# Twelve attention pairs computed in the form of the later ones, with a new order of the matmul blocks around them

## The chip, the cores and the metric

One core of one Trainium2 chip runs the whole program. The metric is device time in microseconds (us) of one execution. TensorE (PE) does the matmuls, VectorE (DVE) and ScalarE (ACT) work on what it leaves in PSUM, GpSimd (POOL) prepares sums of weights, and SyncE (SP) issues nearly all transfers.

## The reference

A windowed attention over 8 batches and 8 heads, then a feed-forward layer with a parametric ReLU on its output. Heads 0 to 3 see the last 32 tokens, heads 4 to 7 every fourth of the last 128.

```python
scores = scale * np.matmul(q, k.transpose(0, 1, 3, 2))      # q, k, v: 8, 8, 576, 64
scores = np.where(masks[None], scores, -1e9)                # plain heads, dilated heads
attn = np.exp(scores - scores.max(-1, keepdims=True))
attn = attn / (attn.sum(-1, keepdims=True) + 1e-9)
x = np.matmul(attn, v)                                      # to 4608 tokens x 512
h = x @ w_in                                                # 512 x 2048
g = np.maximum(h, 0) + alpha * np.minimum(h, 0)
out = g @ w_out                                             # 2048 x 512
```

## The kernel before

**Feed-forward.** Tokens come in nine tiles of 512. Each float32 factor is held as a high and a low part, and a product takes three passes (high by high, high by low, low by high). Tiles 0, 1 and 2 are done in 48 slices (t, f) of one tile by 128 columns of `w_in`; slice n = 0 to 47 is the loop variable of the file's last loops. A slice has two blocks on TensorE, each 12 matmuls of 512 columns: h(n) (`ffn_h`, line 467) and, later, y(n) (`ffn_y`, line 515). Between them stand `ffn_parts` (two DVE instructions that read h from PSUM, lines 487 and 488; for n up to 20 `ffn_sum`, line 480, in their place), `ffn_high` (one ACT cast, line 493) and `ffn_low` (one DVE subtraction, line 498). y(n) reads the high part in its first matmul and the low part from its second on. Slices 6 to 21 are tile 1, 22 to 31 tile 0, 32 to 47 tile 2. Tiles 3 to 8 are done afterwards, two tiles at a time, by `paired_stage`.

**Attention.** A pair is two heads of one batch; pair p = 0 to 31. `scores` puts the products of a pair into two PSUM banks (line 229, or line 253 in the later form), `maxima` masks them and takes row maxima (DVE, lines 288 and 291), `exponentials` is nine ACT instructions (line 301), `divisions` and `turns` normalize and transpose (DVE, lines 308 to 316), `values` multiplies by v (line 333, later form line 278), and `highs` and `lows` copy the result out of PSUM into the token tiles (ACT line 387; DVE lines 392 and 394).

**Two forms.** In the earlier form each quarter of the partitions belongs to one head and one half of the sequence, and the values go to two banks. In the later form (`mixed`, pairs 20 to 31) each quarter takes a run of one head and then a run of the other (`chain`), the values go to four banks, one for each of four runs (`CHAINS`), and the copies out of PSUM are cut by run. Three late pairs (`NARROW`) keep one head on each quarter in that form. The later form has its own masks and its own layout of v.

**Order.** Every engine works through its instructions in the order in which the program issues them. PSUM has eight banks: four "a" banks, handed out in turn by `bank("a", ...)` to h, scores and values, and four "y" banks that collect y for a whole tile. A bank is handed on when its last reader is done. Up to n = 18 DVE and ACT also convert the weights (lines 429 to 448). In the loop of line 1505 pair p = 8 to 19 has its scores at n = 20 + 2(p - 8), its divisions at the next slice and its values at the slice after that (pair 8 one later), so that from n = 24 to 42 the order on TensorE is: h, y, scores, values, h, y. Every second odd slice also splits a sum of weights (`combined_high`, `combined_low`, line 578). From n = 39 on the operands of `paired_stage` are prepared from token tiles 3 and 4 (`token_parts`, lines 659 to 674, put into `late_ops` at 39, 43, 45, 46 and 47). After the loop come y(47), the four copies of tile 2's result (`end`, lines 525 and 527), and `paired_stage`, whose first six matmuls are followed by the scores of pair 20, into two of the y banks just emptied.

Of the kernel before, what the change touches and what calls it, by code (L numbers as in the profile page):

```python
# [18 lines left out]
B, H, S, D = 8, 8, 576, 64  # L19
# [14 lines left out]
NSTD = 3  # L34
NFP = NF // 2
AHEAD = 20
EARLY = 20
NARROW = (27, 28, 31)
GP = 4
# [28 lines left out]
def tile_window_attention_prelu_ffn(  # L68
# [110 lines left out]
    class Pair:  # L179
        def __init__(self, b, c):  # L180
            self.b, self.c = b, c
            p = b * NC + c
            self.onto = p <= NC + 2
            self.small = nc.gpsimd if p <= NC else nc.vector
            self.banks = "y" if self.onto else "a"
            self.late = p == 0
            self.plain = 2 * c < HP
            self.mask = PLAIN if self.plain else DILATED
            self.id = f"{b}_{c}"
            self.pr = spare_pr[p % 2] if b < 2 else pr0  # L190
            self.room = rooms[c] if b < 2 else None
            self.sm = sums[p % 2]
            self.mixed = p >= AHEAD
            self.narrow, self.tags, self.spots = p in NARROW, None, None

        def load_qk(self):
# [9 lines left out]
        def load_v(self):  # L206
            if self.room is None:
                self.v = att.tile([P, HB + 1 + self.mixed, D], F32, tag="v", name=f"v_{self.id}")
            else:
                self.v = self.room[:, 2 * S:taken].rearrange("p (j d) -> p j d", d=D)  # L210
            nc.sync.dma_start(out=self.v, in_=vX[self.b - AHEAD // NC, self.c] if self.mixed else vW[self.b, self.c])

        def scores(self):

# [123 lines left out]
        def places(self):  # L338

            base = self.b * S  # L340
            if self.mixed:
                for n, (first, length) in enumerate(CHAINS):
                    a, last = first * BQ, (first + length) * BQ
                    flat = self.po[n].rearrange("d i q -> d (i q)")
                    while a < last:
                        if self.plain:
                            t = (base + a) // TT
                            z = min(last, (t + 1) * TT - base)
                            to = half(t, self.c)[:, base + a - t * TT:base + z - t * TT]
                        else:  # L350
                            r, i = divmod(a, SEG)
                            t = (base + i * DILATION) // TT
                            z = min(last, r * SEG + min(SEG, ((t + 1) * TT - base) // DILATION))
                            i -= (t * TT - base) // DILATION
                            to = half(t, self.c).rearrange("d (i r) -> d r i", r=DILATION)[:, r, i:i + z - a]
                        yield n % 2, flat[:, a - first * BQ:z - first * BQ], [to]
                        a = z
                return
            for u in range(2):
                flat = self.po[u].rearrange("d i q -> d (i q)")  # L360
                if self.plain:
                    a, end = base + u * HQ, base + (u + 1) * HQ
                    while a < end:
                        t = a // TT
                        z = min(end, (t + 1) * TT)
                        s0 = a - base - u * HQ
                        x, cut = half(t, self.c), slice(a - t * TT, z - t * TT)
                        yield u, flat[:, s0:s0 + z - a], [x[:, e, cut] for e in range(2)] if t < NSTD else [x[:, cut]]
                        a = z
                else:  # L370
                    src = flat.rearrange("d (r i) -> d i r", r=2)
                    a, end = base, base + S
                    while a < end:
                        t = a // TT
                        z = min(end, (t + 1) * TT)
                        i0, i1 = (a - base) // DILATION, (z - base) // DILATION
                        x, cut = half(t, self.c), slice(a - t * TT, z - t * TT)
                        yield u, src[:, i0:i1], [
                            p.rearrange("d (i r) -> d i r", r=DILATION)[:, :, 2 * u:2 * u + 2]
                            for p in ([x[:, e, cut] for e in range(2)] if t < NSTD else [x[:, cut]])]  # L380
                        a = z
# [933 lines left out]
        w.magnitude()  # L1315
        return w

    def masks_of(kind):
        nc.sync.dma_start(out=mask_sb[:, kind:kind + HB], in_=masks[:, kind:kind + HB])

    def behind(t, *lots):

# [97 lines left out]
            load()  # L1420

    sums_early = {}
    loads_early = {CUT - 2: [lambda: masks_of(PLAIN)]}
    for k in range(GP):
        first, last = early_sum(k)
        loads_early[CUT + 4 * k - 3 if k else NC - 1] = [first]
# [66 lines left out]
    for p in range(2 * NC, AHEAD):  # L1493
        n = EARLY + 2 * (p - 2 * NC)
        score_at[n] = pairs[p]
        value_at[n + 3 if p == 2 * NC else n + 2] = pairs[p]
    divide_at = {n + 1: u for n, u in score_at.items()}

    split_at, combine_at = {}, {}
    for k in range(NFP):  # L1500
# [3 lines left out]

    for n in range(CUT, NS):
        scored, valued, divided = (at.get(n) for at in (score_at, value_at, divide_at))
        whole = n + 1 == 2 * NF
        if n + 1 < NS and not whole:
            ffn_h(*slices[n + 1])
        if n <= SECOND - 2:  # L1510

# [5 lines left out]
            for op in words[:1]:  # L1517
                op()
            ffn_low(*slices[n])
            if divided and n < SECOND - 2:  # L1520
                divided.divisions()
                divided.turns()
            for op in words[1:]:
                op()
            if n + 1 <= SECOND - 2:
# [6 lines left out]
                w.high()  # L1532
        elif late:
            late.pop().low()
        if whole:
            ffn_y(*slices[n - 1])
            ffn_h(*slices[n + 1])
        if SECOND - 2 <= n < NS - 1:
            ffn_parts(*slices[n + 1])
            ffn_high(*slices[n + 1])  # L1540
            if divided:
                divided.divisions()
                divided.turns()
            ffn_low(*slices[n + 1])
        if valued is pairs[2 * NC]:
            valued.values()
            valued.highs()
            valued.lows()
        if not whole:
            ffn_y(*slices[n - 1])  # L1550
        if n in split_at:
            combined_high(split_at[n])
        if scored:
            scored.scores()
        if valued and valued is not pairs[2 * NC]:
            valued.values()
        if n in split_at:
            combined_low(split_at[n])
        if scored:
            scored.maxima()  # L1560
            scored.exponentials(0, 5)
        while ended:
            ended.pop()()
        if valued and valued is not pairs[2 * NC]:
            valued.highs()
            valued.lows()
        if scored:
            scored.exponentials(5)
        for u in pairs[2 * NC:AHEAD + 1]:
            if u is pairs[2 * NC]:  # L1570
                due = 2 * (n == SECOND - 4,)
# [11 lines left out]
            combine(combine_at[n], "xB1" if n < SCRATCH + 5 else "xA1")  # L1583
        if n == NS - 9:
            plan_parts()
        if n == NS - 2:
            nc.sync.dma_start(out=mask_sb, in_=masks[:, NMASK:2 * NMASK])
        for op in late_ops.pop(n, ()):
            op()
        if n >= NS - NRING + 2:  # L1590
# [81 lines left out]
```

## Time and profile before

| | |
|---|---|
| median of 3 runs | 846.46 us (846.22 to 846.62) |
| the profiled execution | 846.51 us |
| its span, first to last instruction | 844.3 us |
| PE busy | 828.9 us (98%) |
| DVE busy | 629.7 us (75%) |
| ACT busy | 446.6 us (53%) |

Times in the rows below are counted from the start of that span. A timeline row gives start, duration, engine, line, operation, output <- input, and how many like instructions were merged into it; in square brackets stands idle time ahead of it and who ended it. The duration of a merged row holds the tail of its last matmul, so the pace of TensorE is read from one row's start to the next one's.

### The profile page before, as it was taken

Reading aid. Unit: us, or ns where it says so; the run is one execution under the profiler, and the core shown is the slowest. Engines: PE = TensorE matmul, PEld = TensorE weight load, DVE = VectorE, ACT = ScalarE, POOL = GpSimd, SP = SyncE. Lnnn points to the kernel's source line nnn. Section 1 sums busy time; section 2 is a strip of 40 time slices with the busy share of each in tenths; the row PEclk is TensorE's granted clock in tenths of the full one; section 3 lists DMA queues with packets and bytes.
Section 4 is the critical chain, followed back from the end, with each engine's and each line's share of the span. In section 5 each row is a group of like instructions: output and inputs, shape, how many; then the busy total and the mean of one; then the engine's idle time right before and its main releaser. Section 6 shows DMA issues by size and latency. Waiting matters only on the chain.

```text
span 844.3 us, 20355 instructions
## 1 busy us (share of the span) xinstructions
PE 828.9 (98%) x8071; PEld 675.2 (80%) x8071; DVE 629.7 (75%) x1043; ACT 446.6 (53%) x1234; POOL 126.6 (15%) x146
## 2 busy tenths in 40 slices
PE   8899999999999999999999999999999999999998
PEld 5577888888888888878778888788888888888886
DVE  4988788986767677697645987888379978843983
ACT  6886676444333444566436652666266446634650
POOL 0205154700314350040630000000000000000000
PEclk9999999999999999999999999999999999999999
DMA  7766567635989976577887678767766786667673
GB/s 250 255 200 190 200 224 229 196 103 176 293 268 313 307 229 213 194 218 242 269 306 211 196 215 284 221 194 212 222 168 191 219 265 196 190 197 192 193 216 136
DMA packets 123966, 185.59 MB, mean 220 GB/s; under 512 B 10464, under 2 KB 64352, under 8 KB 123872
## 3 DMA queue, kind: packets, MB, share of 16 engines
q1 hardware_dynamic: 123584, 184.03, 70.8%
q8 instruction: 64, 1.05, 0.5%
q10 hardware_dynamic: 288, 0.26, 0.1%
q14 instruction: 30, 0.25, 0.1%
HBM read 138.12 MB, written 46.14 MB: 218 GB/s over the span
## 4 chain that ended last, share of the span: by engine, by line
PE 90%; DVE 4%; ACT 3%; DMA 2%; issue 1%; SPq 0%; ACTq 0%; DVEq 0%
PE h L467 15%; PE y L515 15%; PE pA L681 14%; PE qA L1118 12%; PE pC L681 7%; PE qC L1118 6%; PE y L964 6%; PE qB L1118 3%; PE pB L681 3%; PE o L333 2%; PE s L229 2%; PE s L253 1%; PE o L278 1%; ACT w_dt.float L301 1%; DMA w_dt.float<-qT 1%
## 5 line engine op out<-in xcount | busy, mean ns | idle before, releaser
L467 PE MATMUL h<-x,w_dt.float32r 128*128 128x512 f32 x576 | 143.0, 397 | 2.1 <-DVE w_dt.float32r L448 1.1
L515 PE MATMUL y<-g,w_dt.float32r 128*128 128x512 f32 x576 | 138.8, 390 | 0.6 <-ACT w_dt.float L301 0.6
L467 PEld LDWEIGHTS h<-x,w_dt.float32r 128*128 128x128 f32 x576 | 107.8, 190 | 26.2 <-DVE w_dt.float32r L448 2.0
L515 PEld LDWEIGHTS y<-g,w_dt.float32r 128*128 128x128 f32 x576 | 107.7, 188 | 23.4 <-ACT w_dt.float L301 1.1
L301 ACT ACTIVATE pr<-pr,nm 128x64 f32<-128x64 f32 x216 | 72.3, 338 | 47.8 <-DVE nm L291 47.8
L493 ACT CAST g<-m 128x512 fp32r<-128x512 f32 x48 | 29.7, 619 | 72.2 <-DVE m L488 68.3
L681 PE MATMUL pA<-parts_w,ring_w 128*128 128x512 f32 x234 | 58.4, 391 | 0.0
L681 PE MATMUL pA<-parts_w,ring_xA 128*128 128x512 f32 x228 | 56.4, 390 | 0.0
L834 DVE TENSOR_TENSOR gp<-stage,gp 128x512 fp32r<-128x512 f32 x80 | 53.5, 683 | 3.4 <-ACT gp L830 3.4
L830 ACT CAST gp<-stage 128x512 fp32r<-128x512 f32 x80 | 46.9, 618 | 9.3 <-DVE stage L827 8.1
L681 PEld LDWEIGHTS pA<-parts_w,ring_w 128*128 128x128 f32 x234 | 43.7, 188 | 9.6 <-ACT stage L723 0.5
L681 PEld LDWEIGHTS pA<-parts_w,ring_xA 128*128 128x128 f32 x228 | 42.6, 188 | 9.0 <-ACT stage L944 0.2
L498 DVE TENSOR_TENSOR g<-m,g 128x512 fp32r<-128x512 f32 x48 | 38.2, 795 | 15.6 <-ACT g L493 15.6
L1118 PE MATMUL qA<-gp,ring_xA 128*128 128x512 f32 x192 | 46.4, 390 | 0.0
L1118 PEld LDWEIGHTS qA<-gp,ring_xA 128*128 128x128 f32 x192 | 35.9, 188 | 7.5
L301 ACT ACTIVATION_READ_ACCUMULATOR pr<-pr,nm 128x1 f32 x216 | 40.9, 189 | 0.0
L1118 PE MATMUL qA<-gp,ring_w 128*128 128x512 f32 x168 | 40.5, 389 | 0.0
L487 DVE TENSOR_SCALAR m<-h,al 128x512 f32<-128x512 f32 x27 | 20.2, 748 | 22.8 <-PE h L467 22.8
L1118 PEld LDWEIGHTS qA<-gp,ring_w 128*128 128x128 f32 x168 | 31.5, 188 | 6.5
L288 DVE SCALAR_TENSOR_TENSOR pr<-s,mask_sb 128x320 f32<-128x320 f32 (+1 forms) x48 | 21.7, 452 | 16.8 <-PE s L253 13.5
L808 DVE TENSOR_TENSOR stage<-pC,stage 128x512 f32<-128x512 f32 x25 | 17.2, 688 | 21.7 <-ACT stage L944 21.7
L1019 DVE TENSOR_TENSOR py<-qA,py 128x512 f32<-128x512 f32 x20 | 13.7, 692 | 20.7 <-PE qA L1118 20.7
(214 smaller groups left out, 1681.6 us busy)
## 6 DMA issues: line engine op xcount, KB each, us to landing
ring_w<-wS SPq DMA_DIRECT2D x68, 256.0 KB, 3.3
ring_xA<-wS SPq DMA_DIRECT2D x67, 256.0 KB, 3.7
ring_g<-wS SPq DMA_DIRECT2D x33, 256.0 KB, 2.8
wO<-w_dt.float32r SPq DMA_DIRECT2D x32, 256.0 KB, 4.7
wS<-wc SPq DMA_DIRECT2D x16, 512.0 KB, 3.6
ring_w<-wO SPq DMA_DIRECT2D x32, 256.0 KB, 3.2
ring_xA<-wY SPq DMA_DIRECT2D x32, 256.0 KB, 3.3
ring_w<-wY SPq DMA_DIRECT2D x32, 256.0 KB, 3.0
```

Of the source, the lines that this page charges most:

```text
L288: nc.vector.scalar_tensor_tensor(out=self.pr[:, a:z], in0=self.ps[i], scalar=SCALE, in1=mask_sb[:, self.mask + a:self.mask + z], op0=ALU.m ...
L301: nc.scalar.activation(out=self.pr[:, r, :], in_=self.ps[r // CUT0][:, r % CUT0, :] if self.onto else self.pr[:, r, :], func=AF.Exp, bias= ...
L467: nc.tensor.matmul(ms[t, f], lhsT=weight(0, a, f)[:, c * P:(c + 1) * P], rhs=half(t, c)[:, e, :], start=(c == 0 and n == 0), stop=(c == NC ...
L487: nc.vector.tensor_scalar(out=m, in0=ps, scalar1=0.0, scalar2=al[:, f:f + 1], op0=ALU.min, op1=ALU.mult)
L493: nc.scalar.copy(out=g[:, 0, :], in_=ms[t, f])
L498: nc.vector.tensor_tensor(out=g[:, 1, :], in0=ms.pop((t, f)), in1=g[:, 0, :].bitcast(F32), op=ALU.subtract)
L515: nc.tensor.matmul(ys[t][c], lhsT=weight(1, a, f)[:, c * P:(c + 1) * P], rhs=g[:, e, :], start=(first and n == 0), stop=(last and n == 2),)
L681: nc.tensor.matmul(to, lhsT=w[:, (2 * a + c) * P:(2 * a + c + 1) * P], rhs=part_of(name, e)[:, c * TT:(c + 1) * TT], start=start and c == ...
L830: nc.scalar.copy(out=self.pair(n)[:, 0], in_=self.whole(n))
L834: nc.vector.tensor_tensor(out=p[:, 1], in0=self.whole(n), in1=p[:, 0].bitcast(F32), op=ALU.subtract)
L964: nc.tensor.matmul(ys2[tt], lhsT=w[:, k * P:(k + 1) * P], rhs=g[:, e], start=j == 0 and n == 0, stop=j == GF - 1 and n == 2)
L1118: nc.tensor.matmul(named(to)[c], lhsT=w[:, b * P:(b + 1) * P], rhs=rhs[:, e], start=begins and k == 0, stop=i == GP - 1 and k == 2, skip_g ...
```

## The change

Pairs 8 to 19 take the later form: `MIXED = 8` takes the place of `AHEAD` where the form is chosen, and `places` writes a high and a low part where the token tile is one of the first three. The masks of that form are loaded at n = 16 and 17; the loads at n = 4 and 46 go. Divisions move to two slices after the scores, values to three after. From n = 20 on an even slice issues y(n-1) ahead of h(n+1) and then the scores; an odd slice issues h(n+1), y(n-1) and then the values.

```diff
+MIXED = 8
-            self.mixed = p >= AHEAD
+            self.mixed = p >= MIXED
...
-            nc.sync.dma_start(out=self.v, in_=vX[self.b - AHEAD // NC, self.c] if self.mixed else vW[self.b, self.c])
+            nc.sync.dma_start(out=self.v, in_=vX[self.b - MIXED // NC, self.c] if self.mixed else vW[self.b, self.c])
...
-                            to = half(t, self.c)[:, base + a - t * TT:base + z - t * TT]
+                            cut = slice(base + a - t * TT, base + z - t * TT)
...
-                            to = half(t, self.c).rearrange("d (i r) -> d r i", r=DILATION)[:, r, i:i + z - a]
-                        yield n % 2, flat[:, a - first * BQ:z - first * BQ], [to]
+                            cut = slice(r + i * DILATION, r + (i + z - a - 1) * DILATION + 1, DILATION)
+                        x = half(t, self.c)
+                        yield n % 2, flat[:, a - first * BQ:z - first * BQ], (
+                            [x[:, e, cut] for e in range(2)] if t < NSTD else [x[:, cut]])
...
-    loads_early = {CUT - 2: [lambda: masks_of(PLAIN)]}
+    loads_early = {EARLY - 4: [lambda: masks_of(PLAIN, NMASK)], EARLY - 3: [lambda: masks_of(DILATED, NMASK)]}
...
-        value_at[n + 3 if p == 2 * NC else n + 2] = pairs[p]
-    divide_at = {n + 1: u for n, u in score_at.items()}
+        value_at[n + 3] = pairs[p]
+    divide_at = {n + 2: u for n, u in score_at.items()}
...
-        whole = n + 1 == 2 * NF
-        if n + 1 < NS and not whole:
+        turned = n >= EARLY and n % 2 == 0
+        if turned:
+            ffn_y(*slices[n - 1])
+        if n + 1 < NS:
             ffn_h(*slices[n + 1])
...
-            if divided and n < SECOND - 2:
-                divided.divisions()
-                divided.turns()
...
-        if whole:
-            ffn_y(*slices[n - 1])
-            ffn_h(*slices[n + 1])
+        while turned and ended:
+            ended.pop()()
+        if divided:
+            divided.divisions()
+            divided.turns()
+        if scored:
+            scored.scores()
         if SECOND - 2 <= n < NS - 1:
             ffn_parts(*slices[n + 1])
             ffn_high(*slices[n + 1])
-            if divided:
-                divided.divisions()
-                divided.turns()
-            ffn_low(*slices[n + 1])
-        if valued is pairs[2 * NC]:
-            valued.values()
-            valued.highs()
-            valued.lows()
-        if not whole:
+            if not scored:
+                ffn_low(*slices[n + 1])
+        if not turned:
             ffn_y(*slices[n - 1])
         if n in split_at:
             combined_high(split_at[n])
+        if valued:
+            valued.values()
         if scored:
-            scored.scores()
-        if valued and valued is not pairs[2 * NC]:
-            valued.values()
+            scored.maxima()
+            ffn_low(*slices[n + 1])
+            scored.exponentials()
+        if valued:
+            valued.highs()
+            valued.lows()
+        while ended:
+            ended.pop()()
         if n in split_at:
             combined_low(split_at[n])
-        if scored:
-            scored.maxima()
-            scored.exponentials(0, 5)
-        while ended:
-            ended.pop()()
-        if valued and valued is not pairs[2 * NC]:
-            valued.highs()
-            valued.lows()
-        if scored:
-            scored.exponentials(5)
...
-        if n == NS - 2:
-            nc.sync.dma_start(out=mask_sb, in_=masks[:, NMASK:2 * NMASK])
```

The rest of the diff is the argument of `masks_of` and the layout of v on the host.

## Rows read from the trace of the kernel before

**Rows 1.** Busy time by stretch: engines, granted clock, share of DMA engines, GB/s

```profile
168.00:322.00 154.00, 154.00 (x2179) 127.42 (x2178) 109.91 (x204) 65.35 (x273) 42.49 (x45) 1.00 0.76 240
322.00:345.00 23.00, 23.00 (x173) 18.95 (x172) 19.59 (x24) 10.38 (x14) 0.00 (x0) 1.00 0.47 149
```

**Rows 2.** Timeline of TensorE, two scores that follow each other, earlier form

```profile
205.37 1.21 PE L229 MATMUL s<-k,q 64*32 64x64 f32 x72
...
218.90 1.21 PE L229 MATMUL s<-k,q 64*32 64x64 f32 x72
```

**Rows 3.** Timeline of TensorE at n = 20 and 21: h(21), y(19), scores, h(22)

```profile
159.89 3.26 PE L467 MATMUL h<-x,w_dt.float32r 128*128 128x512 f32 x12
162.99 2.89 PE L515 MATMUL y<-g,w_dt.float32r 128*128 128x512 f32 x12
165.81 1.21 PE L229 MATMUL s<-k,q 64*32 64x64 f32 x72
166.94 3.03 PE L467 MATMUL h<-x,w_dt.float32r 128*128 128x512 f32 x12
```

**Rows 4.** Timeline of TensorE in `paired_stage`, later form, scores and values apart

```profile
403.85 0.97 PE L253 MATMUL s<-k,q 64*32 64x64 f32 x72
404.75 3.06 PE L964 MATMUL y<-gp,ring_w 128*128 128x512 f32 x12
407.74 1.13 PE L278 MATMUL o<-pt,v 32*64 32x32 f32 x84
408.80 4.37 PE L964 MATMUL y<-gp,ring_xA 128*128 128x512 f32 x18
413.10 0.97 PE L253 MATMUL s<-k,q 64*32 64x64 f32 x72
```

**Rows 5.** The same timeline, the scores of a pair of `NARROW`

```profile
446.20 1.21 PE L253 MATMUL s<-k,q 64*32 64x64 f32 x72
```

**Rows 6.** Timeline of TensorE, values alone at n = 44, and the loop's end

```profile
327.17 1.35 PE L333 MATMUL o<-pt,v 32*64 32x32 f32 x76
328.45 3.01 PE L467 MATMUL h<-x,w_dt.float32r 128*128 128x512 f32 x12
...
336.74 8.32 PE L515 MATMUL y<-g,w_dt.float32r 128*128 128x512 f32 x36
...
346.35 0.97 PE L253 MATMUL s<-k,q 64*32 64x64 f32 x72
```

**Rows 7.** Timeline of DVE: the low part of slice 19

```profile
161.66 0.67 DVE L498 TENSOR_TENSOR g<-m,g 128x512 fp32r<-128x512 f32 x1
```

**Rows 8.** Timeline of TensorE: an h block that stopped after its second matmul

```profile
71.42 0.61 PE L467 MATMUL h<-x,w_dt.float32r 128*128 128x512 f32 x2
73.17 2.56 PE L467 MATMUL h<-x,w_dt.float32r 128*128 128x512 f32 x10 [1.15 <-DVE w_dt.float32r L448]
```

**Rows 9.** Timeline of DVE, n = 43 to the loop's end

```profile
320.51 0.16 DVE L308 TENSOR_TENSOR rs<-sums,tiny 128x9 f32<-128x9 f32 x1
...
322.45 0.65 DVE L498 TENSOR_TENSOR g<-m,g 128x512 fp32r<-128x512 f32 x1
...
324.15 1.22 DVE L666 TENSOR_TENSOR parts_w<-raw_xB,parts_w 128x1024 fp32r<-128x1024 f32 x1
...
328.76 0.75 DVE L487 TENSOR_SCALAR m<-h,al 128x512 f32<-128x512 f32 x1
...
331.53 0.28 DVE L394 COPY raw_xB<-o 128x128 f32<-128x128 f32 x1
...
340.50 0.69 DVE L498 TENSOR_TENSOR g<-m,g 128x512 fp32r<-128x512 f32 x1 [0.76 <-ACT g L493]
...
345.65 1.28 DVE L525 COPY ob<-y 128x512 f32<-128x512 f32 x2
```

**Rows 10.** Timeline of DVE: the five copies of a late dilated pair

```profile
443.36 0.80 DVE L394 COPY raw_xB<-o 128x16 f32<-128x16 f32 x5 [3.81 <-PE o L278]
```

**Rows 11.** The page's costliest groups: masks of a pair, two such instructions each

```profile
L288 DVE SCALAR_TENSOR_TENSOR pr<-s,mask_sb 128x320 f32<-128x320 f32 (+1 forms) x48 | 21.7, 452 | 16.8 <-PE s L253 13.5
```

More of the change, by code (lines that the diff above doesn't have):

```diff
@@ L1316, in conversion, with masks_of @@
         return w
-    def masks_of(kind):
-        nc.sync.dma_start(out=mask_sb[:, kind:kind + HB], in_=masks[:, kind:kind + HB])
+    def masks_of(kind, mixed=0):
+        nc.sync.dma_start(out=mask_sb[:, kind:kind + HB], in_=masks[:, mixed + kind:mixed + kind + HB])
     def behind(t, *lots):
@@ L1643 @@
     vw = v.reshape(B, NC, 2, 2 * HB, BQ, D)[:, :, :, blocks].transpose(0, 1, 2, 3, 5, 4, 6).reshape(B, NC, P, HB + 1, D)
-    blocked = v.reshape(B, NC, 2, 2 * HB, BQ, D)[AHEAD // NC:]
+    blocked = v.reshape(B, NC, 2, 2 * HB, BQ, D)[MIXED // NC:]
     vx, vn = (
@@ L1651 @@
     for p in NARROW:
-        at = p // NC - AHEAD // NC, p % NC
+        at = p // NC - MIXED // NC, p % NC
         vx[at] = vn[at]
```

## The prediction, made before the change was run

> **What bounds the kernel now.** I read the busy times by stretch first. From 168 to 345 us, the stretch in which pairs 8 to 19 run, TensorE is busy all the time, 154.00 of 154.00 us and then 23.00 of 23.00, at full granted clock [rows 1]. So time is won here only by making TensorE's own work shorter, and any new wait of TensorE is lost in full. The second thing to see in the same view is that DVE has 44 us to spare in the first stretch but almost none in the last 23 us of the loop, where it is busy 19.59 us [rows 1]. Then I read TensorE's timeline for the pace and the price of a pair, and DVE's timeline wherever a block is moved nearer to the work that feeds it.
>
> The pace: 36 matmuls from 336.74 to the next row, which by the same timeline starts 1.45 us before 346.35, take 8.16 us, or 0.227 us each [rows 6]. A block of 12 takes 2.72 us.
>
> **A pair on TensorE.** In the earlier form two back-to-back pairs start 13.53 us apart with four blocks (10.88 us) between [rows 2], so scores and values together cost 2.65 us; ten pairs of scores with values stand like that. Scores alone cost 1.13 us [rows 3], values alone 1.28 us [rows 6]. In the later form scores take 0.90, values 1.06 us, and a whole round with 30 matmuls (6.80 us) takes 9.25 us, so a pair costs 2.45 us although its scores and values stand apart [rows 4]. The 12 matmuls between them take 2.99 instead of 2.72 us: 0.27 us to leave small matmuls and come back, a little less around the values. That the gain comes from alternating heads, and not from the call, is seen in a pair that keeps one head on a quarter: its scores last 1.21 us, as in the earlier form, against 0.97 [rows 2, 4, 5].
>
> Now the sum. Before: ten at 2.65 = 26.5; two scores alone at 1.13 + 0.25 and two values alone at 1.28 + 0.25 add 5.8; together 32.3. After: twelve at 2.45 = 29.4. That is **2.9 us saved** (2.8 to 3.0). Four more value matmuls a pair (84 records for 76) are inside the 1.06 us [rows 4, 6].
>
> The split has a price of its own: an extra change between large and small matmuls costs some 0.25 us a pair, 1.13 + 1.28 = 2.41 us alone, 2.65 with one pair of changes, 2.9 with two [rows 2, 3, 6]. The Trainium skill, "TensorEngine Tiling (Array Packing)", section Key Properties, says that a change of tiling mode drains the engine. This trace agrees, and the twelve extra pairs of changes are already in the 2.45; without them the saving would be some 5 us.
>
> **The first turned slice, n = 20.** The old order was y(18), h(21), y(19). The new one puts y(19) straight behind y(18), at 159.89 us, where h(21) stood [rows 3]. But the low part of slice 19 is still queued on DVE behind weight conversions that the change doesn't touch: it starts at 161.66 and ends at 162.33 [rows 7]. y(19) may issue its first matmul and must then wait. A block that stops after some matmuls is seen elsewhere: two issued, then 1.15 us idle until a DVE result came [rows 8]. The second matmul was due at 159.89 + 0.23 = 160.12, so TensorE **loses 2.2 us**. Bounds: 1.8 if DVE runs a little ahead, 2.6 with the handover. What h(21) loses today at the same place, 3.10 us instead of 2.72 [rows 3], goes, since its weights are then long converted: **0.4 us back**.
>
> **The end of the loop.** Here DVE is the engine to follow [rows 1]. Today the low part of slice 47 starts at 340.50, and after it four operand instructions and the copies of y(47) follow; the first copy of the last row, half of 1.28 us, ends at 345.65 + 0.64 = 346.29, and the scores of pair 20, which need that bank, start at 346.35 [rows 6, 9]. There is no slack: what DVE is late there, TensorE waits. The change puts into this queue pair 19's divisions and transposition, which used to be done one slice earlier ahead of the operand work (322.45 - 320.51 = 1.94 us [rows 9]), and moves pair 19's values two blocks later, just ahead of y(45).
>
> I count from the end of pair 18's values. DVE: five copies, 0.15 + 0.80 [rows 10], 0.95; the low part of the weight sum, about 1.13 (of the 1.70 from 322.45 to 324.15), 2.1; the three operand instructions with a cast between, 328.76 - 324.15 = 4.61, 6.7; divisions and transposition, 1.94, 8.6; slice 45's parts, cast and low part, 331.53 - 328.76 = 2.77, 11.4; the two parts instructions of slice 46, about twice 0.75, 12.9 [rows 9]. TensorE by then has done y(43), h(45), h(46) and y(44), 4 x 2.72 + 0.23 = 11.1 us, and wants to start pair 19's values. Their four banks are, in turn, two free ones and those of h(45) and h(46). The last is free only at 12.9. **So TensorE waits 1.8 us** for a bank that the two-bank form didn't need. Values end at 13.9; y(45) and h(47) end at 19.5; DVE, which has meanwhile done three more operand instructions, takes up slice 47 at 19.7, and its low part starts 2.77 - 0.61 = 2.16 later, at 21.9. From there the old distance holds, 346.29 - 340.50 = 5.79: pair 20's scores start at 27.7. Without waits TensorE would be there after eight blocks, six matmuls, the values and four changes: 21.76 + 1.36 + 1.06 + 0.5 = 24.7. **Loss: 3.0 us.** Bounds: 1.3 if the bank is free in time and only DVE's longer queue counts; 3.7 if that queue is later by half a microsecond more.
>
> **The rest.** The masks are now two loads of 295 KB ahead of pair 8's keys and values on SP, instead of one early and a whole one at n = 46. They come behind the last weight loads in the queue, and pair 8's mask is first read some 20 us later; without that cover each would cost its 1.2 us at 240 GB/s [rows 1]. Divisions move to where DVE waits for h anyway, for all pairs but the last. Copies out of PSUM grow from 2 to 3 a side to as many as 9 for pairs 10 and 11 and 5 or 6 for the other dilated pairs; at 0.16 us each [rows 10] they cost DVE under 1.5 us of the 13 us of a round, beside y and h blocks. Both go in at nothing; the price without the cover is the third rival.
>
> **Sum.** 846.51 (the profiled execution; span 844.3 and 2.2 around it; the median is 846.46) - 2.9 - 0.4 + 2.2 + 3.0 = **848.4 us**.
>
> **Rivals.**
>
> *No new wait.* y(19)'s data or the last banks come in time after all, because DVE, with h(21) later and GpSimd's sums behind it, works faster than its rows of today. Then only the saving stands: 846.5 - 3.3 = **843.2**. It decides from the point at which DVE's low part of slice 19 ends before 160.1. Against it: that instruction is queued behind work that is issued in the same order in both kernels. Chance 0.08.
>
> *Only one of the two waits.* With the wait at n = 20 alone, 845.4; with the end of the loop alone, 846.2. For it: my count of the end runs over a dozen queued steps, and half a microsecond of slack in h(46)'s bank would shorten it by about that. Chance 0.22.
>
> *The four banks catch every round.* In a steady round, counted from the end of values, y(n-1) and h(n+1) take 2 x 2.72 and two changes, so slice n+1's parts can start at 5.8 us, the four mask and maximum instructions take some 1.8 [rows 11], the low part 0.6, and slice n+2's parts end at about 11.1; the next values, after scores and two more blocks, start at 12.2. That is a margin of 1.1 us. If DVE is late by more, as it is when GpSimd slows it, each of eleven rounds pays the excess: 0.3 us each gives 848.4 + 3.3 = **851.7**. The Trainium skill, "TensorEngine Tiling (Array Packing)", section PSUM Bottleneck, names this outcome: tiling speeds up TensorE and not the evacuation of PSUM. No row shows it in the loop so far. Chance 0.13.
>
> **How the numbers follow.** Forecast 0.53, rivals 0.08, 0.22 and 0.13, and 0.04 for what I don't see. The forecast's own range, from its bounds, is 846.3 to 849.6. The range of 8 in 10 takes in the second rival below and the light cases of the third above: **845.4 to 850.0**. A measurement of this kernel tells about 0.2% from no change, 1.7 us, so faster is under 844.8 and slower over 848.2. The forecast lies just over that line: three fifths of it, the third rival and half of the unseen are slower, 0.45; the rest of the forecast and the second rival are within, 0.43; the first rival and a remainder are faster, 0.12.
>
> **What would show it.** In the changed kernel's timeline of TensorE: scores of 0.97 and values of 1.13 us for all of pairs 8 to 19; y(19) split after its first matmul with some 2 us idle, released by DVE's low part; a wait in pair 19's values released by the parts of slice 46; a wait before or in pair 20's scores released by a copy of y(47). If TensorE is busy without gaps from 168 to 345 us, the first rival is right; if values wait in many rounds, the third. I am wrong altogether if values in four banks take longer here than in the later stage.

## The result, and the profile after

| | before | after |
|---|---|---|
| median of 4 runs | 846.34 us (845.71 to 846.62) | 856.82 us (856.17 to 858.36) |
| profiled execution | 846.51 us, span 844.3 | 856.63 us, span 854.8 |
| forecast | | 848.4 us (845.4 to 850.0) |

The ratio is **1.0127** (95%: 1.0110 to 1.0145). The kernel became slower, as forecast, but by 10.5 us and not by 2: the time lies outside the range.

The lines that answer to [rows 1], busy time by stretch (PE, PEld, DVE, ACT, POOL, then granted clock, share of the DMA engines, GB/s), in the kernel after:

```profile
168.00:322.00 154.00, 149.00 (x2173) 119.61 (x2168) 112.89 (x218) 62.69 (x277) 47.07 (x48) 0.98 0.76 235
322.00:345.00 23.00, 21.73 (x253) 17.68 (x252) 18.53 (x34) 11.02 (x38) 0.00 (x0) 1.00 0.48 153
```

TensorE, which had no gap in either stretch, now has five microseconds in the first and 1.3 in the second. Where they lie is read from its timeline. First a quiet round, which answers to [rows 2] (scores, then values, then the next scores):

```profile
192.42 0.97 PE L254 MATMUL s<-k,q 64*32 64x64 f32 x72
...
198.99 1.13 PE L279 MATMUL o<-pt,v 32*64 32x32 f32 x84
...
205.71 0.97 PE L254 MATMUL s<-k,q 64*32 64x64 f32 x72
```

A round lasts 13.29 us, against 13.53 in [rows 2]. The new form works, with scores and values as long as in [rows 4].

The two places that the prediction named. At n = 20, which answers to [rows 3, 7] (TensorE, then DVE's low part of slice 19):

```profile
157.06 3.49 PE L518 MATMUL y<-g,w_dt.float32r 128*128 128x512 f32 x13
161.69 2.79 PE L518 MATMUL y<-g,w_dt.float32r 128*128 128x512 f32 x11 [1.14 <-DVE g L501]
```
```profile
160.95 0.68 DVE L501 TENSOR_TENSOR g<-m,g 128x512 fp32r<-128x512 f32 x1
```

And the loop's end, TensorE, which answers to [rows 6]:

```profile
338.28 0.31 PE L279 MATMUL o<-pt,v 32*64 32x32 f32 x6
339.86 1.05 PE L279 MATMUL o<-pt,v 32*64 32x32 f32 x78 [1.27 <-DVE m L491]
...
346.43 5.96 PE L518 MATMUL y<-g,w_dt.float32r 128*128 128x512 f32 x24
352.22 1.52 PE L684 MATMUL pA<-parts_w,ring_w 128*128 128x512 f32 x6
353.67 0.32 PE L254 MATMUL s<-k,q 64*32 64x64 f32 x8
354.74 0.86 PE L254 MATMUL s<-k,q 64*32 64x64 f32 x64 [0.75 <-DVE ob L528]
355.53 1.66 PE L684 MATMUL pC<-parts_w,ring_w 128*128 128x512 f32 x6
```

Both are as described: y(19) stops after its first matmul until the low part is done, pair 19's values stop until h(46)'s bank is read, pair 20's scores until a copy of y(47) is done. A smaller loss stands between the last two: y(46) and y(47) take 5.79 us to the next row, 0.35 more than 24 matmuls at the pace of [rows 6], and in that time a weight load of y(47) waits 0.48 us for DVE's low part of slice 47.

The third place was not in the prediction. TensorE at n = 32 and 33, from the scores of pair 14 to those of pair 15:

```profile
245.57 0.97 PE L254 MATMUL s<-k,q 64*32 64x64 f32 x72
...
249.32 2.88 PE L518 MATMUL y<-g,w_dt.float32r 128*128 128x512 f32 x12
254.51 0.30 PE L279 MATMUL o<-pt,v 32*64 32x32 f32 x4 [2.31 <-DVE pr L289]
255.37 0.30 PE L279 MATMUL o<-pt,v 32*64 32x32 f32 x2 [0.55 <-DVE pr L289]
257.81 1.46 PE L279 MATMUL o<-pt,v 32*64 32x32 f32 x78 [2.14 <-DVE m L491]
259.19 4.54 PE L518 MATMUL y<-g,w_dt.float32r 128*128 128x512 f32 x12
...
266.41 0.97 PE L254 MATMUL s<-k,q 64*32 64x64 f32 x72
```

This round lasts 20.84 us, 7.55 more than a quiet one: 5.00 us of waits, all on DVE, and then a y block of 4.54 instead of 3.02 us. What DVE did in that time:

```profile
247.18 0.69 DVE L526 TENSOR_TENSOR ob<-y,ob 128x512 f32<-128x512 f32 x1 [6.65 <-DMA ob<-part]
248.74 2.03 DVE L526 TENSOR_TENSOR ob<-y,ob 128x512 f32<-128x512 f32 x3 [0.87 <-DMA ob<-part]
250.69 0.16 DVE L309 TENSOR_TENSOR rs<-sums,tiny 128x9 f32<-128x9 f32 x1
...
253.98 0.48 DVE L289 SCALAR_TENSOR_TENSOR pr<-s,mask_sb 128x320 f32<-128x320 f32 x1
...
257.06 0.69 DVE L491 SCALAR_TENSOR_TENSOR m<-h,m 128x512 f32<-128x512 f32 x1
```

The four additions of line 526 are the `end` of tile 0: they add the part of the result that was put into DRAM after slice 5 (`part`) to the y banks. In the new order they are issued in slice 32, ahead of everything else that DVE does in that slice and the next: pair 13's divisions, the parts of slice 33, pair 14's masks, the parts of slice 34. The first of them waits 6.65 us for its load, and then everything behind them is late. The load itself, in the queue of SP:

```profile
242.64 2.29 SPq L516 DMA_DIRECT2D ob<-part  x4
```

It was issued at the same place in the kernel before, with the same median of some 4 us to landing. Before, however, the additions came last on DVE in that slice (the kernel before, queue of SP and timeline of DVE):

```profile
242.97 2.28 SPq L513 DMA_DIRECT2D ob<-part  x4
```
```profile
249.08 2.48 DVE L523 TENSOR_TENSOR ob<-y,ob 128x512 f32<-128x512 f32 x4
```

They started at 249.08, after the load had landed, with no wait. Behind the new wait TensorE's clock falls (busy time by stretch of the kernel after, columns as above):

```profile
248.00:252.00 4.00, 4.00 (x19) 3.15 (x17) 3.16 (x7) 0.00 (x0) 0.00 (x0) 1.00 0.66 242
252.00:256.00 4.00, 0.80 (x7) 0.38 (x6) 3.90 (x8) 1.54 (x7) 0.00 (x0) 0.95 1.02 302
256.00:260.00 4.00, 2.19 (x80) 2.03 (x81) 3.01 (x7) 3.97 (x18) 0.00 (x0) 0.50 0.47 150
260.00:264.00 4.00, 4.00 (x13) 3.14 (x13) 3.66 (x5) 0.00 (x0) 2.94 (x2) 0.69 0.91 272
```

The clock stands at 0.50, the lower of its two levels (1.2 of 2.4 GHz), when the values resume after five microseconds with little work. The y block behind them takes 1.52 us more than in a quiet round, and the values, in three pieces, take the rest of the 7.55.

Last, one wait of another kind, far behind the loop, in `paired_stage`:

```profile
440.94 0.85 PE L967 MATMUL y<-gp,ring_w 128*128 128x512 f32 x3 [1.79 <-issue]
```

**The account.** From y(18) to the scores of pair 20, after minus before, by the starts of the rows.

| stretch | before | after | difference |
|---|---|---|---|
| y(18) to the scores of pair 8 (n = 20) | 8.64 | 10.07 | +1.43 |
| pair 8's scores to pair 20's, less the two rows below | 180.54 | 177.48 | -3.06 |
| round of n = 32 and 33, over 13.29 | | 7.55 | +7.55 |
| pair 19's values to y(45), over 1.05 in a quiet round | | 1.51 | +1.51 |
| first to second set of matmuls of `paired_stage`, with pair 20's scores between | 2.35 | 3.31 | +0.96 |

The sum is +8.39, y(18) itself started 0.11 earlier, and the matmuls after pair 20's scores are 8.28 us late in the trace (355.53 against 347.25). The 1.79 us of "issue" bring it to 10.1. The two profiled executions differ by 10.12 us and their spans by 10.5 (854.8 against 844.3), so some 0.4 us of the span have no place in this table. The second row, -3.06, also holds the 0.35 us that y(47) loses: the twelve pairs save 3.4 us.

### The profile page after: what moved, and what is told of

The parts are those of the page before. It is cut to its first block, busy times and chain, and to the rows that moved or that the text cites. A ratio compares the mean times of both kernels' runs of the same rounds, so it can differ in the third digit from the quotient of the medians.

```text
span 854.8 us, 20630 instructions
## 1 busy us (share of the span) xinstructions
PE 828.4 (97%) x8167; PEld 670.1 (78%) x8167; DVE 634.6 (74%) x1073; ACT 448.3 (52%) x1268; POOL 126.3 (15%) x146
## 4 chain that ended last, share of the span: by engine, by line
PE 78%; DVE 11%; DMA 4%; ACT 3%; issue 2%; SPq 1%; ACTq 0%; DVEq 0%
PE pA L684 14%; PE qA L1121 12%; PE h L470 10%; PE y L518 9%; PE pC L684 7%; PE qC L1121 6%; PE y L967 5%; PE pB L684 3%; PE qB L1121 3%; PE o L279 3%; PE s L254 2%; DVE w_dt.float32r L451 2%; DVE wa L440 1%; DMA wW<-wa 1%; DVE g L501 1%
## 5 line engine op out<-in xcount | busy, mean ns | idle before, releaser
L518 PE MATMUL y<-g,w_dt.float32r 128*128 128x512 f32 x576 | 142.4, 396 | 2.1 <-DVE g L501 1.1
L470 PE MATMUL h<-x,w_dt.float32r 128*128 128x512 f32 x576 | 141.0, 393 | 2.0 <-DVE w_dt.float32r L451 1.1
L279 PEld LDWEIGHTS o<-pt,v 32*64 32x64 f32 x1764 | 22.2, 134 | 14.1 <-issue 6.7
```

Of the source, the lines that this page charges most:

```text
L279: nc.tensor.matmul(self.po[c][e * D:(e + 1) * D, a:z, :], lhsT=self.v[rows, (CUT0 + 1) * s + i, :], rhs=self.pt[rows, (r + a) * BK + (BQ i ...
L470: nc.tensor.matmul(ms[t, f], lhsT=weight(0, a, f)[:, c * P:(c + 1) * P], rhs=half(t, c)[:, e, :], start=(c == 0 and n == 0), stop=(c == NC ...
L518: nc.tensor.matmul(ys[t][c], lhsT=weight(1, a, f)[:, c * P:(c + 1) * P], rhs=g[:, e, :], start=(first and n == 0), stop=(last and n == 2),)
```

## Experiments

My theory after the result: the saving, y(19) and the loop's end are as predicted, and 7.5 us of what is missing are the four additions, late by their transfer. Rivals: the four banks of the values are short of room in any round that is disturbed (the prediction's third rival), or the turned slice 32 costs by itself. The kernel before doesn't take the same time on every chip, so each run is compared with its time beside that run, by the ratio; the times in the expectations start from the 856.8 us above.

**Slice 32 left in the old order.** y(31) comes after h(33) again, and the additions come last again.

```diff
-        turned = n >= EARLY and n % 2 == 0
+        turned = n >= EARLY and n % 2 == 0 and n != 2 * NF
```

> The changed kernel, with the old order at n = 32 alone: h(33), scores, y(31), and the four additions that close tile 0 stand on DVE behind the scores' maxima instead of ahead of the divisions. Theory A (late operand): the wait of pair 13's values at n = 33 comes from DVE, which stands at the additions until the stored part of tile 0 arrives, 6.6 us; moved behind, they hold nobody up: the wait of some 5 us and the half clock after it go, 7 to 7.5 us in all, so about 849.3 us. Theory B (four banks): values into four banks wait for slice n+2's parts anyway, DVE's margin is too small; some 2 us or more of the wait stay, 851 to 855 us.

Measured: 847.68 us against 844.38 of before, ratio 1.0044 (1.0026 to 1.0061). No wait at n = 33; the two rounds around slice 32 take 27.0 us together, 0.4 more than twice 13.29, 0.34 of it a wait of h(33) for one of ACT's copies. The waits of y(19) and of the loop's end stay. So the loss sits in slice 32's order. In this profile the clock fell at the loop's end instead, behind a wait that in the kernel after had no such sequel (its timeline of TensorE):

```profile
330.54 1.05 PE L279 MATMUL o<-pt,v 32*64 32x32 f32 x78 [1.27 <-DVE m L491]
331.51 4.63 PE L518 MATMUL y<-g,w_dt.float32r 128*128 128x512 f32 x12
```

The same wait of 1.27 us stands in the rows of the loop's end above, and there the y block behind it takes 3.03 us.

**The loads left out.** Order and instructions stay, but the additions take a second operand that is already in SBUF.

```diff
-            if rest:
-                nc.sync.dma_start(out=o[c], in_=part[c])
...
-                    nc.vector.tensor_tensor(out=o[c], in0=ys[t][c], in1=o[c], op=ALU.add)
+                    nc.vector.tensor_tensor(out=o[c], in0=ys[t][c], in1=half(2, c)[:, 0, :].bitcast(F32), op=ALU.add)
```

> The changed kernel in its own order, but the four additions that close tile 0 add a value that lies in SBUF already instead of the stored part: its first six slices are left out of tile 0's result and four transfers of 256 KB fall away; DVE's four additions stay where they are. Theory A (late operand): the additions run as soon as y(31)'s banks are done, the wait at n = 33 goes, 849 to 849.5 us. Theory B (four banks) or a theory that the 2.7 us of additions alone upset DVE's order: 2 us or more of the wait stay, 851 us or more.

Measured: 847.41 us against 844.38 of before, ratio 1.0045 (1.0027 to 1.0064). DVE and TensorE in that profile:

```profile
239.65 2.74 DVE L524 TENSOR_TENSOR ob<-y,x 128x512 f32<-128x512 f32 x4 [0.37 <-PE y L516]
```
```profile
244.31 0.97 PE L254 MATMUL s<-k,q 64*32 64x64 f32 x72
...
250.88 1.12 PE L279 MATMUL o<-pt,v 32*64 32x32 f32 x84
...
257.60 0.97 PE L254 MATMUL s<-k,q 64*32 64x64 f32 x72
```

The additions stand at the same place of the queue and cost nothing: the round is 13.29 us, values in one piece. It is the late operand, not the place alone and not the four banks (the transfers are gone here too; the next run keeps them). The kernel is 3.0 us behind the one before all the same, and the other terms of the account give only 0.8. In this profile the difference stands at n = 20 (TensorE):

```profile
157.31 0.50 PE L516 MATMUL y<-g,w_dt.float32r 128*128 128x512 f32 x1 [0.61 <-ACT g L496]
158.82 4.38 PE L516 MATMUL y<-g,w_dt.float32r 128*128 128x512 f32 x11 [1.00 <-DVE g L501]
```

Here y(19) also waits for its high part, and behind its waits the clock falls (0.62 from 158 to 162 us): 11 matmuls last 4.38 us, 2.79 in the kernel after. From y(18) to pair 8's scores it is 12.05 us, 2.0 more than there.

**The loads issued one slice earlier.** Nothing is left out.

```diff
+        if (t, f) == (0, NF - 2):
+            obs[t] = [ffp.tile([P, TT], F32, tag="m", name=f"ob_{t}_{NF - 1}_{c}", bufs=5) for c in range(NC)]
+            for c in range(NC):
+                nc.sync.dma_start(out=obs[t][c], in_=part[c])
...
-            if rest:
-                nc.sync.dma_start(out=o[c], in_=part[c])
```

> The changed kernel with nothing left out and its order kept, but the four loads of the rows saved in DRAM are issued one slice earlier, with y(30) instead of y(31). Theory (the additions of tile 0 are late by their loads' transfer alone): no wait and no half clock at n = 33, rounds of 13.29 us there; the waits of y(19), 1.7 us, and of the loop's end, 2.4 us, stay: 1.003 to 1.005 of before, as with the loads left out. Rival (the place ahead of DVE's queue costs by itself, whatever the loads do): some of the 5.4 us of waits stay at n = 33, 1.008 or more.

Measured: 849.6 us against 844.81 of before, ratio 1.0059 (1.0038 to 1.0080), with a wait left that the theory had not expected. Queue of SP, DVE and TensorE:

```profile
239.10 2.92 SPq L519 DMA_DIRECT2D ob<-part  x4
```
```profile
245.13 2.70 DVE L530 TENSOR_TENSOR ob<-y,ob 128x512 f32<-128x512 f32 x4 [3.33 <-DMA ob<-part]
```
```profile
254.87 1.05 PE L279 MATMUL o<-pt,v 32*64 32x32 f32 x78 [1.15 <-DVE m L491]
```

The loads are issued behind the transfers that SP has in that slice, at 239.10, and the first addition can start only 6 us later. So the additions still wait, 3.33 us, and TensorE 1.15. Together these kernels give the size of the effect. From the end of the last addition to the end of slice 34's parts DVE needs 6.98 us in both the kernel after (250.77 to 257.75) and this one (247.83 to 254.81). The additions ended 5.20 us after the start of pair 14's scores in the kernel after, 0.99 after it here (scores at 246.84), 1.92 before it with the loads left out; TensorE waited 5.00, 1.15 and 0. Three more profiles with the additions in this place fit: 4.81 us after the scores and 4.46 of waits (operands earlier, below), 5.20 and 4.96 (the unchanged kernel once more), 6.58 and 6.04 (y(19) in its old place). The additions have to end by the time the scores start, and each microsecond beyond that is about one of TensorE's. In this profile, too, the clock falls at n = 20 (the same 11 matmuls last 4.38 us), which is part of why it is 4.8 us behind.

**y(19) left in its old place.**

```diff
-        turned = n >= EARLY and n % 2 == 0
+        turned = n > EARLY and n % 2 == 0
```

> The changed kernel, with the old order at n = 20 alone: h(21) ahead of y(19). If y(19)'s wait for the low part of slice 19 (second matmul due at 160.0, issued at 161.7 in the changed kernel) is lost in full, its 1.7 us go and the 0.4 us that h(21) loses for its weights come back: 1.3 us faster than the changed kernel, 855.5 us. If that wait is only shifted, because the next blocks would wait for the same late DVE, there is no change, 856.8 us.

Measured: 854.95 us against 844.38 of before, ratio 1.0136 (1.0121 to 1.0152): against the unchanged kernel no difference that these intervals tell apart. y(19)'s wait is gone, but h(21) is late again:

```profile
160.91 3.29 PE L470 MATMUL h<-x,w_dt.float32r 128*128 128x512 f32 x12 [0.59 <-ACT w_dt.float32r L448]
```

From y(18) to h(22) it is 10.44 us, 10.97 in the kernel after, 9.77 before. Undoing this part saves 0.5 us in this execution, not the 1.2 by which the kernel after is behind there, since h(21)'s weights come late again as in [rows 3].

**Operands of the loop's end earlier.** Two operand instructions, a cast on ACT and a subtraction on DVE, move from n = 43 to 41, so that DVE's queue is shorter where pair 19's values want h(46)'s bank.

```diff
-        late_ops[NS - 5] = zeroth[2:] + first
+        late_ops[NS - 7] = zeroth[2:]
+        late_ops[NS - 5] = first
```

> The changed kernel, with one of the operand preparations (the cast and the low part of B21, one DVE instruction of 1.2 us) moved from n = 43 to n = 41. If the waits at the end of the loop (1.3 us in pair 19's values, 0.4 in y(47), 0.8 in pair 20's scores) come from DVE's queue, the first goes nearly and the others shrink: 1.1 to 1.5 us faster than the changed kernel, 855.5 us. If the values wait for the banks for another reason than the queue (the order of banks and blocks alone), there is no change, 856.8 us.

Measured: 854.08 us against 844.38 of before, ratio 1.0124 (1.0107 to 1.0141). Pair 19's values in that profile:

```profile
339.01 1.50 PE L279 MATMUL o<-pt,v 32*64 32x32 f32 x84
```

The next block starts 1.42 us after their start (340.43) instead of 2.56 (338.28 to 340.84), so that wait was indeed DVE's queue. The wait of pair 20's scores stays at 0.75 us. The gain of 1.1 us is seen in the trace; in the times it is lost in the spread.

**The unchanged kernel once more,** on the chip of the next two.

> The changed kernel unchanged, on the chip of the other runs of this call. The waits that follow from queues must be there again: about 1.7 us in y(19), about 5 us in pair 13's values at n = 33 with half clock behind it, 1.3 and 0.75 us at the end of the loop. The 1.8 us in which TensorE waited in the later stage for nothing that the profile shows, seen once, may be gone: if it belongs to the change, it stands in the same block again; if it is chance, it doesn't. Ratio to the kernel before 1.011 to 1.0145 as measured.

Measured: 855.36 us against 845.12 of before, ratio 1.0129 (1.0109 to 1.0148). The waits at n = 20 (0.29 us for the high part, 1.00 for the low), at n = 33 (4.96) and at the loop's end (1.27 and 0.75) are there with nearly the same lengths. The 1.79 us of "issue" in `paired_stage` are not: it was seen in one execution only, and nothing ties it to the change. But here the clock falls at the loop's end:

```profile
341.82 1.05 PE L279 MATMUL o<-pt,v 32*64 32x32 f32 x78 [1.27 <-DVE m L491]
342.80 4.61 PE L518 MATMUL y<-g,w_dt.float32r 128*128 128x512 f32 x12
```

From y(18) to the end of the span the two profiles of this kernel take 697.7 and 698.5 us, that of before 687.1: they lose 10.6 and 11.3, some 2 us of it in different places.

**The form without the order.** The later form for pairs 8 to 19, but in the order of before; maxima are put ahead of the values, so that the banks of the scores can be read.

```diff
-        value_at[n + 3] = pairs[p]
-    divide_at = {n + 2: u for n, u in score_at.items()}
+        value_at[n + 3 if p == 2 * NC else n + 2] = pairs[p]
+    divide_at = {n + 1: u for n, u in score_at.items()}
...
+            scored.scores()
+            scored.maxima()
+        if valued and valued is not pairs[2 * NC]:
+            valued.values()
```

> The kernel before, with the later form for pairs 8 to 19 and the old order of blocks (only the maxima of a pair are issued ahead of the values, which need the same banks). Theory: scores and values get shorter by 0.45 us a pair, but the values' third and fourth bank are those of the scores just computed, and DVE's masks have read the second only 2.2 us after the scores began, where the values would want it after 0.95: each of ten rounds waits 1.2 us. In sum some 5 us saved and 12 lost, 6 to 8 us slower than the kernel before, ratio 1.007 to 1.01. If four banks cost nothing in the old order, it is 5 us faster, ratio 0.994.

Measured: 884.0 us against 845.12 of before, ratio 1.0456 (1.0436 to 1.0476), far above what was expected. A round of that profile, TensorE:

```profile
211.62 0.97 PE L254 MATMUL s<-k,q 64*32 64x64 f32 x72
...
213.18 0.30 PE L279 MATMUL o<-pt,v 32*64 32x32 f32 x2 [0.35 <-DVE pr L289]
214.03 1.05 PE L279 MATMUL o<-pt,v 32*64 32x32 f32 x78 [0.56 <-DVE pr L289]
216.42 2.99 PE L470 MATMUL h<-x,w_dt.float32r 128*128 128x512 f32 x12 [1.34 <-ACT x L390]
...
227.50 0.97 PE L254 MATMUL s<-k,q 64*32 64x64 f32 x72
```

15.88 us. Scores take two of the four "a" banks and the values right behind them need all four: they wait 0.91 us for the masks, and the next h waits 1.34 us until ACT has copied values out of its bank. The wait for the masks, 0.9 us or more, stands in each of the ten rounds; that for the copies in nine, from 0.65 to 1.34 us. In six of them the clock falls behind it, and the longest round takes 18.5 us (227.50 to 246.04). The Trainium skill, "TensorEngine Tiling (Array Packing)", section PSUM Bottleneck, says that TensorE gets faster by tiling and the evacuation of PSUM does not; in this order the trace agrees, with masks and copies waited for as above. In the new order, at 13.29 us a round, TensorE waits for neither. So the form needs the order: two blocks between scores and values, and two behind the values, cover the copies.

**The order without the form.** The order of after, pairs 8 to 19 in the earlier form.

```diff
-MIXED = 8
+MIXED = AHEAD
```

> The changed kernel's order with the earlier form (two banks) for pairs 8 to 19, and the old mask loads. Scores and values stand apart at their old lengths: 0.26 us more a round, 2.6 us. y(19) waits as in the changed kernel, 1.3 us net. At n = 33 DVE is as late as in the changed kernel, but two banks wait only for slice 33's parts and the first mask of pair 14, not for slice 34's parts: a wait of about 3 us instead of 5 to 5.6. At the loop's end pair 19's values find their banks free: no wait there, but 1 to 1.7 us before pair 20's scores. In sum 7 to 9 us slower than the kernel before, ratio 1.008 to 1.011. If the wait at n = 33 is as long as with four banks, the form has no part in it.

Measured: 853.8 us against 845.12 of before, ratio 1.0102 (1.0081 to 1.0123). TensorE, two scores of a quiet stretch, and the values at n = 33:

```profile
205.23 1.21 PE L230 MATMUL s<-k,q 64*32 64x64 f32 x72
...
219.00 1.21 PE L230 MATMUL s<-k,q 64*32 64x64 f32 x72
...
255.72 1.35 PE L334 MATMUL o<-pt,v 32*64 32x32 f32 x76 [2.30 <-DVE pr L289]
```

Three things come out of this. A round takes 13.77 us: the split of scores and values costs 0.24 us a pair (13.53 in [rows 2]), and the form gives back 0.48 (to 13.29). The wait at n = 33 is there too, but only its first part, 2.30 us; the values in two banks don't need the bank of h(34), and so the 2.7 us that follow it in the kernel after belong to the four banks. Pair 19's values don't wait at all, while pair 20's scores wait the same 0.75 us: the first of the two waits at the loop's end belongs to the form, the second to the order.

**All three places mended.** y(19) and slice 32 in the old order, the two operand instructions at n = 41, and the four copies of y(47) on ScalarE.

```diff
-                elif c % 2:
+                elif c % 2 and t != 2:
...
-        late_ops[NS - 5] = zeroth[2:] + first
+        late_ops[NS - 7] = zeroth[2:]
+        late_ops[NS - 5] = first
...
-        turned = n >= EARLY and n % 2 == 0
+        turned = n > EARLY and n % 2 == 0 and n != 2 * NF
```

> The changed kernel with its three waits mended: the old order at n = 20 and n = 32, B21 prepared at n = 41, and the four copies of y(47) all on ScalarE, so that the banks of pair 20's scores don't wait for DVE. If the waits explain the loss, TensorE's shorter scores and values (2.9 us) remain but for some 0.7 us at the loop's end: 1.5 to 2.5 us faster than the kernel before, ratio 0.997 to 0.998. If DVE's longer queue costs time elsewhere, it is no faster, ratio 1.000 or more.

Measured: 843.81 us against 845.12 of before beside it, ratio **0.9985** (0.9974 to 0.9996). With the next kernel it is the best of these and a little faster than before, by less than the 1.5 to 2.5 us expected. What is left of the waits in its profile, TensorE:

```profile
328.35 1.49 PE L279 MATMUL o<-pt,v 32*64 32x32 f32 x84
...
342.59 0.97 PE L254 MATMUL s<-k,q 64*32 64x64 f32 x72
```

Pair 20's scores are in one piece again. From h(21) to them it is 184.68 us (h(21) starts at 157.91), against 186.46 of before: 1.8 us won, which is the 3.1 of the account (y(47) loses its 0.35 here too) less 0.4 in pair 19's values, 0.4 in the two rounds around slice 32, and some 0.4 by rounds of 13.33 instead of 13.29 us. The profiled span, 841.4, is 2.9 under that of before, but h(21) started 2 us earlier for reasons that lie ahead of the change, so the 1.8 is the change's share in this profile; the medians differ by 1.3.

**All mended, slice 32 in the new order,** with the loads one slice earlier.

```diff
-        turned = n > EARLY and n % 2 == 0 and n != 2 * NF
+        turned = n > EARLY and n % 2 == 0
```

> The three mends together (y(19) left in its old place, tile 2's first loads one slice earlier, all four copies of y(47) on ScalarE), but slice 32 in the new order with the four DRAM loads one slice earlier. Theory: TensorE has no wait in the loop and takes the 2.9 us of the form: 0.997 to 0.9995, as with slice 32 left in the old order. Rival (the new order at slice 32 has a price of its own): 1.001 or more, with a wait at n = 33.

Measured: 843.58 us against 844.81 of before, ratio 0.9988 (0.9973 to 1.0003). The wait at n = 33 is 1.03 us, with the additions ending 0.88 us after the start of pair 14's scores, in line with the relation above; the kernel with slice 32 in the old order has no such wait but loses 0.4 us in the two rounds around it. The times don't tell the two apart.

## Why the prediction was wrong

**The saving on TensorE, 2.9 us: right in kind, 3.4 in size.** The account's 3.06 and y(47)'s 0.35 make 3.4, above the stated 2.8 to 3.0: in the loop a pair costs 2.41 us (13.29 less four blocks), not the 2.45 read from [rows 4]. Its two halves were right: 0.24 us a pair paid for the split and 0.48 gained by the form. The count of twelve extra pairs of changes is two too many, since two of the twelve pairs stood apart before the change.

**y(19): right, and somewhat smaller.** The mechanism is the one described, with the same releaser. The second matmul came 1.7 us late instead of 2.2, because DVE's low part ended at 161.63 and not at 162.33; with h(21)'s 0.4 the net is +1.4 against +1.8.

**The loop's end: right, and somewhat smaller.** 1.27 us of wait for h(46)'s bank against 1.8, then y(47) and the scores of pair 20; together 1.51 + 0.35 + 0.96 = 2.8 us against 3.0.

These three give 846.5 - 3.4 + 1.4 + 2.8 = 847.3, or 0.8 us more than before. That the kernel without the loads took 847.41 us is no proof of this sum: beside it the kernel before took 844.38, so it was 3.0 us behind, 2.0 of them by the longer waits and the lower clock at n = 20 in its profile. The nearness of the two numbers is chance.

**What failed is the part called "The rest".** It listed divisions, masks and copies out of PSUM as what the new order moves on DVE, put them at nothing, and left out `end`, which cost 7.55 us. The diff has it in plain sight: `while turned and ended: ended.pop()()` stands ahead of the divisions, the scores and the parts. In the loop this runs twice, at n = 22 for tile 1, where it is copies alone, and at n = 32 for tile 0, whose `end` reads from DRAM. The step that was missing is the one for a moved instruction: what does it wait for, and who is queued behind it? The rows for it were in the trace of before. The loads are issued at 242.97 and take some 4 us, the additions stand at 249.08; moved ahead of everything else in slice 32 they can't start before 247, and end at 249.6, while the scores on TensorE start at some 245.6. By the relation shown above that is a wait of about 4 us, and 5.0 was measured. The other 2.5 us, by the clock and the split values, could not have been read from the stretches of [rows 1], where the clock is full throughout; the premise that a new wait is lost in full was too mild here.

**The rivals.** "No new wait" and "Only one of two waits" fall, since both waits are there. "Four banks catch every round" falls too: quiet rounds have no wait, with the additions' loads left out none has from n = 22 to 42, and the rival's margin of 1.1 us is enough. But it named what makes the late additions dear: with two banks their wait costs 2.30 us, with four 5.00. And in the old order, which the rival didn't consider, it decides everything: 0.9 to 2.25 us of waits in each round, and the clock behind them.

**Open.** Some 2 of the 10.5 us have no fixed place: in the first profile they are mostly the 1.79 us of "issue", in the second profile of the same kernel mostly the clock at the loop's end, and the other executions have no profile. Why the clock falls after a wait of 1.27 us in one execution and not in another of the same kernel isn't settled by these runs; what is shown is that it does, and its price.

## What to carry to other kernels

When a change reorders a loop, list every instruction that moves on each in-order engine, one-time work at a tile's end included, and ask of each whether its operands have landed by the new time. An instruction that used to be last in a slice can hide a transfer of some 4 us for nothing; put first, it makes the whole queue wait. Where an extra order is needed only for steady rounds, leave the odd slices as they were: with two slices back in the old order and two mends at the loop's end the same change went from 1.3% slower to 0.15% faster.

## What the runs showed of the hardware

A short wait can cost more than its length, but doesn't always. The wait of 1.27 us at the loop's end stands in six profiles. In three (the kernel after, loads left out, loads earlier) the y block behind it takes 3.01 to 3.03 us; in three (the unchanged kernel once more, slice 32 in the old order, y(19) in its old place) it takes 4.60 to 4.63, with the granted clock at 0.66 from 344 to 348 us of the first of these. Behind y(19)'s wait of 1.00 to 1.26 us for its low part the clock fell in two profiles of seven (loads left out, loads earlier). Behind the wait at n = 33 it fell in each of the four profiles that have it at full length (the kernel after twice, y(19) in its old place, operands earlier). That is some 1.6 us a time.

It may be part of why kernels with waits spread: with the loads left out nine runs took 845.6 to 852.8 us, and the two slowest have the lowest mean granted clocks, 0.991 and 0.993. This is not shown: 7 us is more than the clock costs at these places, and the start of y(18), which lies ahead of the change, alone moves between 153.8 and 158.0 us from profile to profile.

One wait of TensorE on "issue" of 1.79 us in `paired_stage` showed in one of the twelve profiles and in none of the others.
